# One visit instead of two for the state products of a chunk, and a copy of C shared by two engines, in a fused Mamba-2 and gated feed-forward kernel

## The chip, the cores and the metric

The kernel runs on one core of a Trainium2 chip. The metric is the device time of one execution in microseconds. The core has five engines that work at the same time, each through its own queue in order: TensorE (PE in the profile; its weight loads are listed as PEld), VectorE (DVE), ScalarE (ACT), GpSimd (POOL) and SyncE (SP), which issues the DMAs. They wait for one another through semaphores. Matrix products go to PSUM[...]; VectorE and ScalarE read them from there.

## The reference, cut to what matters

A state-space scan over 4 sequences with 8 heads, 768 steps, head size 32 and state size 16 feeds a feed-forward stage over 3072 tokens of width 256, whose middle has 2048 columns. All values are float32.

```
for each chunk of the sequence, with la = log(clip(a)), cum = cumsum(la):
    M       = (C @ B.T) * exp(cum_i - cum_j) * causal
    y       = M @ x  +  (C @ state) * exp(cum_i)
    state   = exp(sum la) * state + sum_j (B_j x_j) * exp(cum_last - cum_j)
X   = y laid out as (tokens, heads * head_dim)
h   = X @ w_in
out = (h * cos(h)) @ w_out
```

## The kernel before, in words

The sequences are cut into six chunks of 128 steps. Chunks 0 and 1 of this cut are handled in half chunks of 64 steps at the start (functions that end in `0` or `_unit`); chunks 2 to 5 are handled whole by `turn2`, `intra2`, `masked`, `open2`, `finish2` and `carry`. In the text, chunk c means one of these whole chunks.

The feed-forward stage sets the pace. It runs in 96 steps n, 16 for each chunk (`NF = 16`); step n of chunk n // 16 takes 256 columns of the middle layer for half of the tokens. One step is a chain through four engines:

- `first(n)`, L725 (8 matmul records): `hp` = y times `w_in`, into a PSUM bank.
- `wind_k(n)`, L732 on ScalarE, and `wind_w(n)`, L738 on VectorE: the argument of the cosine, reduced to one period. Both read `hp`.
- `gate(n)`, L747 on ScalarE: the cosine. `gated(n)`, L752 on VectorE: `gT` = `hp` times the cosine. It is the last reader of `hp`.
- `differ(n)`, L777, L779, L780 on GpSimd: differences of `gT` for a seven-product scheme; then `second(n)`, L834 (14 matmul records): products with `w_out`, summed in PSUM. It is issued two steps later (`LAG = 2`).

`hp` has two PSUM buffers of its own from step 4 on (`bank([P, TB], "hp", tag)` with tag "h" and `bufs=2`): step n writes the buffer of step n - 2, so `first(n)` can start only when `gated(n - 2)` is done.

The order on each engine is the order of the calls in the program (`manual_schedule`): nothing is moved by a scheduler, and an instruction that waits holds all behind it on its engine. In the loop over n (L1067) one turn issues `first(n)`, `wind(n)`, `gate(n)`, then `gated(n)` with some scan work for VectorE before or behind it (the list `behind`), then what TensorE does for the scan, with `second(n - 2)` in between.

The scan work of chunk c is spread over the 16 steps ahead of it. Called by step within those 16:

- steps 8 and 12: `intra2` (L621), the products C times B of two sequences each, into two PSUM tiles of two banks (`pair`, tag "scan", `bufs=2`), and `masked` for one sequence (L640: four VectorE products of these with the decays).
- steps 9 and 13: `masked` for the other sequence, the first entry of `behind`; it stands ahead of `gated` of its step.
- step 14: `open2(c)`, L651 and L659, after `second(12)`: the old state times C into the y tiles, and the sums for the new state. Its y tiles are the same two `pair` buffers. Chunk 5 has no L659, since no chunk comes after it.
- step 15: `finish2(c)`, L675, between `first(15)` and `second(13)`: the masked products times x, added in the y tiles; then `yT` is copied out by ScalarE (L682), and `carry` (L697 on VectorE, L701 on GpSimd) makes the new state.
- the next step, `first` of chunk c's own step 0, reads `yT`.

So TensorE's order around the change, with the step within the 16, is: `first(14)`, `second(12)`, `open2`, `first(15)`, `finish2`, `second(13)`, then `first` of the next chunk. `open2` and `finish2` use small tiles of the array (`tile_position`), the feed-forward products the whole of it.

In the set-up of chunk 0, C is loaded by four DMAs into `c4`, GpSimd copies it in another order of elements into `c0` (L365, 128 partitions x 512 elements), TensorE transposes `c0` in four parts (L417), and ScalarE takes the transposes out of PSUM (L421); the first products C times B (L478) follow. `c0[:, r]` is the operand of the transpose r.

Of the kernel before, what the change touches and what calls it, by code (L numbers as in the profile page):

```python
# [25 lines left out]
def kernel(  # L26
# [13 lines left out]
    V, ACT, G, PE = nc.vector, nc.scalar, nc.gpsimd, nc.tensor  # L40
# [31 lines left out]
    def pair(name):  # L72

        return psum.tile([P, 2, 4 * P], FP32, tag="scan", bufs=2, name=name)
# [44 lines left out]
    c4 = both[0][:, 1].rearrange("p (h r) n -> p h r n", h=H)  # L119
# [23 lines left out]
    def group(q, b):  # L143
        return slice(32 * (q ^ b % 2), 32 * (q ^ b % 2) + 32)
# [52 lines left out]
    def load_along(c, seqs=range(NB)):  # L197
# [5 lines left out]
        for b in seqs:  # L203
            for q in range(4 if b % 2 else 1):
# [9 lines left out]
                      in_=a[:, :, 0:P].rearrange("b h (k i) -> (b h) k i", k=2))  # L214
# [85 lines left out]
    for s in range(2):  # L300
# [3 lines left out]
        out=a_in, in_=a.rearrange("(u b) h (c p) -> (b h c) u p", u=NU, p=P))  # L304
# [52 lines left out]
    for p in range(2):  # L357
# [4 lines left out]
                  in_=mine.unsqueeze(2).to_broadcast([P, H, N]))  # L362
    c0 = loads.tile([P, 2, 2, 4, 2, N], FP32, tag="blocks", name="c0").rearrange(
        "p a b c d n -> p (a b c d n)").rearrange("p (r h n) -> p r h n", r=4, h=H)
    G.tensor_copy(out=c0.rearrange("p r h n -> p h r n"), in_=c4)  # L365
    G.memset(lead, 0.0)
    G.memset(lead[:, :, 0:1], 1.0)
    slot = const.tile([P, 2], FP32, name="slot")
# [275 lines left out]
    def open2(c):  # L644

        ys[c] = y = [pair("y") for _ in range(2)]
        for u in range(2):
            for s in range(2):
                for q in range(4):
                    r, p = group(q, s), 64 * (q % 2)  # L650
                    PE.matmul(y[s][p:p + 64, q // 2, u * P:(u + 1) * P],  # L651
                              lhsT=state[c - 1, u][r, s].rearrange("p t d -> p (t d)"),
                              rhs=part[c, u][2][r, s], start=(u == 0), stop=False,
                              tile_position=(r.start, p), skip_group_check=True)
        for b in range(NB if c < NC - 1 else 0):
            x_, sc = raw[c][1], scaled.pop((c, b))
            for q in range(4):
                two_, r = slice(2 * q, 2 * q + 2), group(q, b)
                PE.matmul(y[0][r, 0, (4 + b) * W:(5 + b) * W],  # L659
                          lhsT=sc[:, two_].rearrange("p h n -> p (h n)"),  # L660
                          rhs=x_[:, b, two_].rearrange("p h d -> p (h d)"), start=False, stop=True,
                          tile_position=(0, r.start), skip_group_check=True)

    def finish2(c):

        xr, y = raw[c][1], ys.pop(c)
        for late in (1, 0):
            i = slice(W, P) if late else slice(0, W)
            for u in range(2):
                for t in range(2):  # L670
                    for s in range(2):
                        b, m = 2 * u + s, part[c, u][1][s]
                        js = slice(0, P) if late else slice(s * W, s * W + W)
                        for q in range(4):
                            PE.matmul(y[s][32 * q:32 * q + 32, t, u * P + i.start:u * P + i.stop],  # L675
                                      lhsT=xr[js, b, 4 * t + q], rhs=m[js, 4 * t + q, i],
                                      start=False, stop=True, tile_position=(js.start, 32 * q),
                                      skip_group_check=True)
        yT[c] = two.tile([P, 2, TB], FP32, tag="yT", name="yT")
        to_ = yT[c].rearrange("p t (u s i) -> p t s u i", u=2, s=2)  # L680
        for s in range(2):
            ACT.copy(out=to_[:, :, s],  # L682
                     in_=y[s][:, :, 0:2 * P].rearrange("p t (u i) -> p t u i", u=2))
        for u in range(2):
            del part[c, u]
            if c < NC - 1:
                carry(c, u, y[0][:, 0, 4 * W:].rearrange("p (u s d) -> p u s d", u=2, s=2)[:, u])

    def carry(c, u, s_ps):


        state[c, u] = new = states.tile([P, 2, 2, D], FP32, tag="state", name="state")
        mask = slot.unsqueeze(1).unsqueeze(3).to_broadcast([P, 2, 2, D])
        whole = scan.tile([P, 2, 2, D], FP32, tag="whole", bufs=1, name="whole")
        old = state.pop((c - 1, u))
        for s in range(2):
            V.scalar_tensor_tensor(out=whole[:, s], in0=old[:, s],  # L697
                                   scalar=reach[c, u][:, s, P - 1:P],
                                   in1=s_ps[:, s].rearrange("p (t d) -> p t d", t=2),
                                   op0=ALU.mult, op1=ALU.add)  # L700
        G.tensor_tensor(out=new, in0=whole, in1=mask, op=ALU.mult)  # L701
# [39 lines left out]
    def wind(n):  # L741
        wind_k(n)
        wind_w(n)
# [172 lines left out]
    take_s0, _ = finish0(0)  # L916
# [47 lines left out]
    def units_at(n, i):  # L964
        return [k for k, at in unit_at.items() if at[i] == n]
# [38 lines left out]
    def ends(n):  # L1004
        return [(c, us) for c, at, us, _, _, end in plan if at + end == n]
# [61 lines left out]
    for n in range(AHEAD, NC * NF + LAG):  # L1067
        c, f = divmod(n, NF)
        if n < NC * NF:

            if c > 0 and f == (NJ if c == 1 else 0):
                if c == 1:
                    load(2, only=(x,))
                load(c + 2)
            if n in (NF - 4, NF + 1):
                for b in range(2):
                    load_a(2, (2 * (n > NF) + b,))
                    load_along(2, (2 * (n > NF) + b,))
            first(n)
            wind(n)  # L1080
            for at in pairs(n):
                turn2(*at)
            for k in units_at(n, 2):
                turn_unit(k)
            if n + 1 in piece:
                rests_of.append(grade(*piece[n + 1], later=True))
            gate(n)
            while len(rests_of) > (n == AHEAD):
                rest = rests_of.pop(0)
                if rest:  # L1090
                    rest()
            joins = n in piece and piece[n] in held
            if joins:
                join(*piece[n])

            behind = [lambda at=at: halved(*at) for at in halves_at(n)]
            behind += [lambda k=k, p=p: decays0(k, p) for k, at in unit_at.items()
                       for p in range(2) if at[0][p] == n]
            behind = [lambda at=(c, 2 * u + 1): masked(*at) for c, u in pairs(n - 2)] + behind
            behind = [lambda k=k: weights(k, 1) for k in units_at(n - 1, 3)] + behind  # L1100
            if not joins and behind:
                behind.pop(0)()
            gated(n)
            if add_s and (n == NF - 5 or units_at(n - 1, 4)):
                add_s()
                add_s = None
            for do in behind:
                do()
            if f not in (10, 11):
                for do in unsummed:  # L1110
                    do()
                unsummed.clear()
            for k, ((_, last_), *_) in unit_at.items():
                if last_ == n:
                    weigh0(k)
                    if k == 3:
                        units_of_decay()
        for i, js in differ_at.get(n, ()):
            differ_w(i, js)
        for c, _ in ends(n - 1):  # L1120
            finish2(c)
            raw.pop(c)
        if n == AHEAD + 1:
            second(AHEAD - LAG)
        if n >= LAG and n != AHEAD:
            second(n - LAG)
        for c, u in pairs(n - 1):
            intra2(c, u)
            masked(c, 2 * u)
        for k in units_at(n, 3):  # L1130
            for t in range(2):
                inner(k, t)
            weights(k, 0)
        for k in units_at(n, 4):
            take_s, add_s = finish0(k)
            take_s()
        for k in units_at(n, 1):
            reach_unit(k)
        for c, _ in ends(n):
            open2(c)  # L1140
        for c, u in pairs(n + 1):
            for b in (2 * u, 2 * u + 1):
                reaches(c, b)
                load_along(c + 1, (b,))
            turn_blocks(c, u)
        for at, (c, u) in block_loads.items():
            if at == n:
                loading = load_blocks(c, u)
            if at <= n < at + 6:
                next(loading)  # L1150
# [30 lines left out]
```

## Time and profile before

| what | value |
|---|---|
| time, median of 3 runs | 371.13 us (370.97 to 371.22) |
| time of the profiled execution | 371.16 us |
| its span, first to last instruction | 369.4 us |
| PE busy / PEld busy | 362.5 us (98%) / 325.0 us (88%) |
| DVE / ACT / POOL busy | 276.9 (75%) / 172.2 (47%) / 213.4 us (58%) |
| L725 `hp` matmuls, x768 | 183.2 us busy |
| L752 `gT`, x96 | 680 ns each |
| L640 `m`, x64 | 411 ns each (median) |

The span is what the trace covers; the time has 1.8 us more around it. A line of a timeline gives start, length, engine, line of code, operation, tile written and tiles read, and, in brackets, how long the engine was idle before it and what ended that. A line of the chain of waits gives start, length and engine of one piece of the chain that ended last. TensorE matmuls overlap one another by a part of their length, so distances between starts say more than lengths.

### The profile page before, as it was taken

What the parts mean: (1) busy time and instruction counts of PE and PEld (TensorE: products, weight loads), DVE (VectorE), ACT (ScalarE), POOL (GpSimd) and SP (SyncE); (2) the same over time, 40 slices, a digit from 0 to 9 for tenths busy, and PEclk for the clock granted to TensorE, in tenths of its full rate; (3) what the DMA queues carried; (4) which work ended last, traced back from release to release, by engine and by line L of the source; (5) the groups of instructions that cost most, each with busy time, mean ns of one, the idle gap of its engine ahead of it and who ended that gap; (6) DMA issues with size and microseconds to landing.
All of it is one profiled execution on the core that took longest, in us unless ns stands there. A gap on an engine that the chain in (4) does not pass through costs nothing.

```text
span 369.4 us, 9265 instructions
## 1 busy us (share of the span) xinstructions
PE 362.5 (98%) x3646; PEld 325.0 (88%) x3646; DVE 276.9 (75%) x451; ACT 172.2 (47%) x299; POOL 213.4 (58%) x336
## 2 busy tenths in 40 slices
PE   7999999999999999999999999999999999999995
PEld 5688888888999889899989999889999988999995
DVE  7789998578699857978876987776887783543463
ACT  2697766453445244354344344434434534444442
POOL 6567757579784456665446674544675344554451
PEclk9999999999999999999999999999999999999999
DMA  9996957257226736631055341020010010010011
GB/s 135 244 381 134 224 114 100 44 147 185 72 78 90 139 106 91 196 107 34 6 80 113 92 129 44 1 52 5 18 23 0 2 30 2 2 29 2 0 30 30
DMA packets 97708, 30.60 MB, mean 83 GB/s; under 512 B 71456, under 2 KB 93568, under 8 KB 97664
## 3 DMA queue, kind: packets, MB, share of 16 engines
q1 hardware_dynamic: 95376, 29.55, 35.0%
q10 hardware_dynamic: 2288, 0.46, 0.8%
q8 instruction: 29, 0.48, 0.5%
q14 instruction: 15, 0.12, 0.1%
HBM read 26.58 MB, written 3.34 MB: 81 GB/s over the span
## 4 chain that ended last, share of the span: by engine, by line
PE 92%; DVE 3%; ACT 2%; issue 1%; ACTq 0%; DVEq 0%
PE hp L725 43%; PE o L834 34%; PE o L796 6%; PE y L675 2%; PE g L621 2%; DVE mag L279 1%; PE g L478 1%; DVE lam L397 1%; PE warm L84 1%; PE y L651 1%; PE y L520 1%; DVE mag L281 1%; PE y L503 1%; DVE w L738 1%; PE a_ps L386 1%
## 5 line engine op out<-in xcount | busy, mean ns | idle before, releaser
L725 PE MATMUL hp<-yT,w_in 128*128 128x256 f32 x768 | 183.2, 382 | 0.4 <-DVE gT L752 0.3
L725 PEld LDWEIGHTS hp<-yT,w_in 128*128 128x128 f32 x768 | 139.4, 190 | 19.5 <-issue 2.3
L777 POOL TENSOR_TENSOR gd<-gT 128x256 f32<-128x256 f32 x79 | 59.9, 758 | 99.9 <-DVE gT L752 86.8
L747 ACT ACTIVATE w<-w,quarter 128x512 f32<-128x512 f32 x96 | 69.2, 721 | 84.4 <-DVE w L738 84.3
L738 DVE SCALAR_TENSOR_TENSOR w<-hp,k 128x512 f32<-128x512 f32 x96 | 65.8, 685 | 44.3 <-ACT k L732 43.9
L732 ACT ACTIVATE k<-hp 128x512 int32<-128x512 f32 x96 | 57.0, 594 | 83.2 <-PE hp L725 82.9
L752 DVE TENSOR_TENSOR gT<-hp,w 128x512 f32<-128x512 f32 x96 | 65.3, 680 | 33.2 <-ACT w L747 21.7
L834 PE MATMUL o<-words,gd 128*128 128x128 f32 x474 | 66.0, 275 | 0.0
L834 PEld LDWEIGHTS o<-words,gd 128*128 128x128 f32 x474 | 59.3, 192 | 0.3 <-POOL gd L779 0.2
L834 PEld LDWEIGHTS o<-w_out,gT 128*128 128x128 f32 x316 | 47.2, 191 | 4.2
L834 PE MATMUL o<-w_out,gT 128*128 128x128 f32 x316 | 48.4, 276 | 0.0
L779 POOL TENSOR_TENSOR gd<-gT,gd 128x128 f32<-128x128 f32 x79 | 44.0, 556 | 6.2
L780 POOL TENSOR_TENSOR gd<-gT,gd 128x128 f32<-128x128 f32 x79 | 43.3, 548 | 6.2
L580 DVE TENSOR_TENSOR_SCAN lam<-arow,unit 128x512 f32<-128x512 f32 x32 | 42.7, 1333 | 0.0
L834 PE MATMUL o<-words,gT 128*128 128x128 f32 x158 | 30.6, 275 | 0.0
L834 PE MATMUL o<-w_out,gd 128*128 128x128 f32 x158 | 30.5, 275 | 0.0
L796 PE MATMUL o<-w_out,gT 128*128 128x256 f32 x128 | 29.9, 379 | 0.0
L796 PEld LDWEIGHTS o<-w_out,gT 128*128 128x128 f32 x128 | 24.2, 190 | 3.3
L640 DVE TENSOR_TENSOR m<-g,lam 128x256 f32<-128x256 f32 x64 | 24.7, 414 | 0.4
L834 PEld LDWEIGHTS o<-words,gT 128*128 128x128 f32 x158 | 24.0, 192 | 0.0
L834 PEld LDWEIGHTS o<-w_out,gd 128*128 128x128 f32 x158 | 24.0, 192 | 0.0
L851 DVE TENSOR_TENSOR sum<-ps,sum 128x256 f32<-128x256 f32 (+1 forms) x27 | 16.7, 645 | 0.6
(111 smaller groups left out, 279.2 us busy)
## 6 DMA issues: line engine op xcount, KB each, us to landing
arow<-a_cut SPq DMA_DIRECT2D x16, 512.0 KB
words<-in_moe_w_in_dram SPq DMA_DIRECT2D x8, 512.0 KB
words<-in_moe_w_out_dram SPq DMA_DIRECT2D x8, 512.0 KB
out_dram<-sum SPq DMA_DIRECT2D x18, 128.0 KB
xr<-in_x_dram SPq DMA_DIRECT2D x16, 128.0 KB
xr<-in_x_dram SPq DMA_DIRECT2D x16, 64.0 KB
bc<-in_B_dram SPq DMA_DIRECT2D x15, 64.0 KB
arow<-a_cut SPq DMA_DIRECT2D x2, 256.0 KB
```

The costliest lines, as they stand in the source:

```text
L580: V.tensor_tensor_scan(out=lam[c, b][:, hs].rearrange("p h i -> p (h i)"), data0=rows_.rearrange("p h i -> p (h i)"), data1=unit[:, b % 2 ...
L640: V.tensor_tensor(out=m_[js, :, :, is_], in0=g_[js, :, :, is_], in1=l_[js, :, :, is_], op=ALU.mult)
L725: PE.matmul(to_[:, e], lhsT=w_in[:, k, fs], rhs=y[:, k], start=(k == 0), stop=(k == KT - 1), skip_group_check=True)
L732: ACT.activation(k, hp[n], AF.Copy, bias=0.25, scale=INV_2PI)
L738: V.scalar_tensor_tensor(out=w, in0=hp[n], scalar=INV_2PI, in1=k, op0=ALU.mult, op1=ALU.subtract)
L747: ACT.activation(cos, cos, AF.Sin, bias=quarter, scale=TWO_PI)
L752: V.tensor_tensor(out=gT[n], in0=hp.pop(n), in1=cos, op=ALU.mult)
L777: G.tensor_tensor(out=d[:, 0:2], in0=g[:, 1:2].to_broadcast([P, 2, P]), in1=g[:, 3::-3], op=ALU.subtract)
L779: G.tensor_tensor(out=d[:, 2], in0=g[:, 0], in1=d[:, 0], op=ALU.subtract)
L780: G.tensor_tensor(out=d[:, 3], in0=g[:, 2], in1=d[:, 2], op=ALU.subtract)
L796: PE.matmul(o[c, u][:, t], lhsT=g[:, 2 * e + t], rhs=w_out[:, 2 * j + e], start=(j == e == t == 0), stop=(j == NJ - 1 and e == 1), skip_gr ...
L834: PE.matmul(at[q], lhsT=a_[q], rhs=w[q], start=(j == 0 and q in starts), stop=(j == NJ - 1), skip_group_check=True)
```

## The change

Two edits.

1. In chunk 0's set-up, the copy `c4` to `c0` is cut in two along r: GpSimd copies r = 0 and 1, ScalarE r = 2 and 3 (128 x 256 elements each).
2. In the loop, `open2(c)` is called one step later, directly ahead of `finish2(c)`: TensorE's order becomes `first(14)`, `second(12)`, `first(15)`, `open2`, `finish2`, `second(13)`. This holds for chunks 2 to 5, four times in all. What `open2` computes, its tiles and buffers, and the order on the other engines stay as they are.

```diff
-    G.tensor_copy(out=c0.rearrange("p r h n -> p h r n"), in_=c4)
+    G.tensor_copy(out=c0[:, 0:2].rearrange("p r h n -> p h r n"), in_=c4[:, :, 0:2])
+    ACT.copy(out=c0[:, 2:4].rearrange("p r h n -> p h r n"), in_=c4[:, :, 2:4])
...
         for c, _ in ends(n - 1):
+            open2(c)
             finish2(c)
             raw.pop(c)
...
-        for c, _ in ends(n):
-            open2(c)
```

## The prediction, on record before the change was run

> **What bounds the kernel now.** I read the page first, then the chain of waits, then the timeline of each engine around the places that are edited. Part 1 of the page:
>
> ```profile
> PE 362.5 (98%) x3646; PEld 325.0 (88%) x3646; DVE 276.9 (75%) x451; ACT 172.2 (47%) x299; POOL 213.4 (58%) x336
> ```
>
> TensorE is the bound, and the chain is TensorE alone from 34.79 us to the end but for splinters. So a TensorE instruction saved is time saved, and a TensorE wait added is time lost. The chain around one visit (chunk 3; start, length):
>
> ```profile
> 183.77 1.73 PE hp L725 x8
> 185.50 1.56 PE o L834 x14
> 187.06 0.62 PE y L651 x32
> 187.68 0.58 PE y L659 x32
> 188.26 1.92 PE hp L725 x8
> 190.19 1.82 PE y L675 x117
> 192.01 1.76 PE o L834 x14
> 193.76 1.30 PE hp L725 x6
> ```
>
> In order: `first(14)`, `second(12)`, `open2` (L651, L659), `first(15)`, `finish2` (L675), `second(13)`, `first` of the next chunk. See that an hp or o block costs 1.73 or 1.56 us, but 1.92 and 1.76 us when small-tile products came just before it: 0.19 and 0.20 us more for each return to the full array, twice a chunk. That is what one visit can save.
>
> Then I asked whether `first(15)` could start where `open2` starts now. Its PSUM buffer is freed by `gated(13)`. VectorE in the same stretch:
>
> ```profile
> 183.12 1.40 DVE L640 TENSOR_TENSOR m<-g,lam 128x256 f32<-128x256 f32 x4
> 184.44 0.67 DVE L738 SCALAR_TENSOR_TENSOR w<-hp,k 128x512 f32<-128x512 f32 x1
> 185.04 1.74 DVE L640 TENSOR_TENSOR m<-g,lam 128x256 f32<-128x256 f32 x4
> 186.81 0.69 DVE L752 TENSOR_TENSOR gT<-hp,w 128x512 f32<-128x512 f32 x1
> 187.42 0.68 DVE L738 SCALAR_TENSOR_TENSOR w<-hp,k 128x512 f32<-128x512 f32 x1
> ```
>
> These are `masked` of the third sequence, w of step 13, `masked` of the fourth, `gated(13)`, w of step 14. `gated(13)` ends at 186.81 + 0.69 = 187.50 us. VectorE has no idle time between 180.25 and 188.1, so it is late by its own load (before these come four L851 sums, 2.3 us). TensorE ends `second(12)` at 187.06: today `open2` fills the time until the buffer is free, and `first(15)` finds it free 0.7 us before its start.
>
> What such a wait looks like is seen once, at the end of the start phase:
>
> ```profile
> 33.97 0.68 DVE L752 TENSOR_TENSOR gT<-hp,w 128x512 f32<-128x512 f32 x1
> 34.79 1.97 PE L725 MATMUL hp<-yT,w_in 128*128 128x256 f32 x8 [0.34 <-DVE gT L752]
> ```
>
> hp starts 0.14 us after gT's end at 34.65, and its block takes 1.97 us from idle. (A second case: gT ends at 151.45, hp starts at 151.60.)
>
> The first edit concerns this stretch:
>
> ```profile
> 6.62 0.61 POOL L365 COPY c<-bc 128x512 f32<-128x512 f32 x1 [0.84 <-DMA bc<-in_C_dram]
> 7.29 0.66 PE L417 MATMUL tp<-ident,c 128*128 128x128 f32 x4 [0.50 <-POOL c L365]
> 7.98 0.84 ACT L421 ACTIVATE cT<-tp,slot 128x256 f32<-128x256 f32 x2 [3.33 <-DVE lam L397]
> 8.71 0.37 ACT L432 COPY turned<-tp 128x256 f32<-128x256 f32 x1
> 9.14 0.73 PE L478 MATMUL g<-cT,turned 32*64 32x128 f32 x32 [0.54 <-ACT turned L432]
> ```
>
> The copy waits for C, the transposes for the copy, and ScalarE has stood idle for 3.3 us when the transposes end at 7.95. The page names DVE lam (ended 7.96) as what released ScalarE; the code has ScalarE need only `slot`, done at 4.0, and the transposes, so I take it as a coincidence.
>
> **What the Trainium skill says.** "TensorEngine Tiling (Array Packing)", Key Properties: changing the tiling mode, as opposed to the tile, drains TensorE. The trace agrees: the 0.19 and 0.20 us above. "Perfetto Trace Analysis", Optimizing Tensor Performance, Matmuls: independent groups should rotate through different PSUM banks so that the evacuation of one overlaps the matmuls of the next. Here hp rotates through two, and the overlap lasts only while VectorE is less than two steps behind; 34.79 shows it end. "TensorE: Matmul & The Clock Gate", Why this matters for your kernels: idle gaps above about 3 us lower the clock. The gaps that I forecast are near 1 us, and the granted clock is 1.00 in all four stretches around the visits, so I charge nothing for it. "ScalarE: Activation LUTs", What ACT_TABLE_LOAD costs: an ACTIVATE with immediate scale and bias takes 186 ns + 0.833 ns per element, an estimate of 0.40 us for 256; the trace has 0.37 us for L432 of that shape.
>
> **The change, part by part.**
>
> *Merging, without any wait.* Chunk 3 takes from the end of `second(12)`: 1.20 (open2) + 1.92 + 1.82 + 1.76 = 6.70 us. In the new order hp follows a full-array block and costs 1.73: 1.73 + 1.20 + 1.82 + 1.76 = 6.51. Gain 0.19 us a chunk, 0.8 us for four.
>
> *The wait it adds.* `first(15)` would start near 187.06 but has to wait for `gated(13)`: 187.50 + 0.14 = 187.64. From there 1.97 + 1.20 + 1.82 + 1.76 ends at 194.39, against 193.76: 0.63 us lost. Queued behind the waiting hp on TensorE are `open2`, `finish2` and `second(13)`, all of which could run but stand behind it. The lower bound: read by starts, hp at 187.50 + 0.06 (a shorter release; L651 in chunk 2 resumes 0.07 us after the VectorE product that it waits for), then 1.73, 0.10 to enter the small tiles, 1.20, 1.82 and 1.66 give 194.07 against hp at 193.60: 0.47. I take 0.56.
>
> *Chunk 4* has the same times 58.12 us later (`gated(13)` ends at 245.62, the next chunk's hp starts at 251.72): 0.47 to 0.63, I take 0.56.
>
> *Chunk 5* has no L659. `gated(13)` ends at 303.75; 303.89 + 1.97 + 0.62 + 1.82 + 1.76 = 310.06 against 309.44 in the chain: 0.62, by starts 0.48; I take 0.55. Here hp starts today 0.14 us after gT: its 0.62 us of L651 lies wholly in time that TensorE would otherwise wait.
>
> *Chunk 2*: `gated(13)` ends later, at 129.00, since VectorE comes in with more scans. 129.14 + 1.97 + 1.20 + 1.82 + 1.76 = 135.89 against 135.13: 0.76, by starts 0.62; I take 0.69. That `open2` today waits 0.32 us within itself, for a y buffer that `masked` frees at 128.28, is in these figures: in the new order that wait is gone, covered by the longer one.
>
> Sum: 0.69 + 0.56 + 0.56 + 0.55 = 2.36 us, bounds 2.04 to 2.64.
>
> *What else moves.* VectorE, ScalarE, GpSimd and SP keep their order. After `finish2` ScalarE copies yT (1.05 us); k and the cosine of step 15 are now done before `finish2` ends, so the copies start at once and end some 1.2 us after `second(13)` starts, which lasts 1.66: covered, with about 0.3 us to spare after the 0.14 us release. `masked` of the fourth sequence is done at 186.78 in chunk 3 (128.28 in chunk 2), before hp can start, so `finish2` doesn't wait for it. The `sc` buffers that L659 now frees later are next written at 198.18 (L563 on GpSimd): no one waits. `open2` issues no DMA; the loads of x and B that reuse buffers wait for `finish2`, as before. One recovery is possible: in chunk 2's own steps hp stalls by 0.18 us at 151.60 (gT late) and an o block by 0.26 us behind it; VectorE is paced by hp there, so I give nothing, and keep -0.4 for the range.
>
> *The shared copy.* GpSimd takes 0.29 us for 128 elements (L361) and 0.61 for 512, so by the line between them 0.40 for 256; ScalarE 0.37 to 0.40, and it is free from 4.65 on. Both wait for the same C. Both halves are done at 6.62 + 0.40 = 7.02, not 7.23: 0.21 us earlier. From there to 34.79 the chain runs through the first products, VectorE and ScalarE, with ScalarE and VectorE rather than a transfer ending nearly every wait (the one DMA wait, ACT for the first weights at 9.32, is 0.2 us). I take 0.20 of gain, bounds 0 (DVE lam was the true releaser, or the gain is lost in the weight conversion up to 34.79) and 0.25. A loss is excluded within 0.05 us, as both copies are shorter than the one they replace.
>
> Total: 2.36 - 0.20 = +2.16 us. The profiled run took 371.16 (span 369.4 and 1.8 around it), which agrees with the median 371.13 within 0.03: **373.3 us**, slower by 0.6%.
>
> **The rivals.** *The wait isn't there* (faster). It would need `gated(13)` done 0.14 us before `second(12)` ends, at 186.92 rather than 187.50, 0.58 us earlier. For it: VectorE is paced by k of earlier steps, and TensorE changes its order. Against it: the order changes only after VectorE's work in question has its inputs, and VectorE is busy without a break from 180.25. Then 4 x 0.19 + 0.20 = 0.96 is gained: 370.2 us. The break-even is hp at about 187.2 in chunk 3. *The wait is partly regained*: the next chunk's stalls vanish (0.44 us in chunk 2) and the later visits have VectorE 0.4 us earlier relative to TensorE, so that each loses 0.1: 0.3 + 3 x 0.1 - 0.2 = +0.4: 371.5 us. Against it: VectorE waits for k in each chunk, so it follows TensorE. *A further wait behind the visit*: hp of the next chunk waits for yT because the copies start late; each 0.4 us beyond the spare 0.3, four times: 373.3 + 1.6 = 374.9. Against it: ScalarE has nothing else to do at that time.
>
> **How the numbers follow.** Forecast 0.80; wait not there 0.09; partly regained 0.05; further wait 0.06. A measurement of this kernel tells about 0.2% (0.74 us) from no change. The forecast's own bounds: low 2.04 - 0.25 - 0.4 = +1.4, 372.5; high 2.64 with no gain at the start and 0.07 us more release for each, +2.9, 374.1. With a little to the lower side for a partial recovery, the range is 372.3 to 374.1. Slower 0.86, within 0.2% 0.05, faster 0.09.
>
> **What would show it.** In the profile after: hp of step 15 in chunks 2 to 5 with an idle time before it ended by DVE gT, near 0.6 us in chunks 3 to 5 and 1.3 us in chunk 2; L651, L659 and L675 in one block; PE's busy time lower by about 0.8 us with a longer span; the transposes L417 near 7.08. The forecast is wrong if hp of step 15 starts within 0.1 us of the end of `second(12)`, or if the distance between the hp starts around a visit (8.27 us from `second(12)` to the next chunk's hp in chunk 3) becomes shorter.

## The result, and the profile after

The changed kernel takes 375.71 us (median of 6 runs, 374.36 to 378.85), the kernel before 371.06 us (6 runs, 370.83 to 371.77). The ratio is 1.0131, with an interval of 1.0092 to 1.017: slower, as forecast, but by 4.65 us where 2.2 us were forecast, and outside the range of 372.3 to 374.1 us. The profiled execution took 375.99 us with a span of 374.1 us, and the span is what is taken apart below. After the change the lines of the code stand one lower (hp is L726, gT L753, `open2` L652 and L660, `finish2` L676, `second` L835), since the copy takes two lines, L365 and L366.

Part 1 of the page after:

```profile
PE 361.9 (97%) x3646; PEld 324.7 (87%) x3646; DVE 275.7 (74%) x451; ACT 173.0 (46%) x300; POOL 217.6 (58%) x336
```

TensorE has 0.6 us less to do and the span is 4.7 us longer. So the loss is idle time. What TensorE waits for, in us in total, times and longest, stands in the table of waits (the three largest lines):

```profile
PE hp L726 <- DVE gT L753: 3.3, 5, 1.2
PE y L676 <- issue: 1.7, 1, 1.7
PE hp L726 <- issue: 1.4, 1, 1.4
```

The first line is the forecast wait: four visits, and the fifth is the one at the end of the start phase, which was there before. The other two lines were not forecast. "issue" means that the profile shows nothing that TensorE waited for.

The chain around chunk 3's visit, after (start, length, piece):

```profile
188.06 0.70 DVE gT L753
188.77 0.14 issue
188.90 1.96 PE hp L726 x8
190.87 0.62 PE y L652 x32
191.49 0.58 PE y L660 x32
192.07 1.68 PE y L676 x117
193.76 1.76 PE o L835 x14
195.51 1.73 PE hp L726 x8
```

Read it against the chain of before: `open2` and `finish2` are one block now, one of the two dear returns to the full array is gone, and the chain leaves TensorE for `gated(13)`, which ends 0.14 us before hp starts. VectorE in the same stretch is the same row of work as before, still without a gap:

```profile
186.31 1.72 DVE L641 TENSOR_TENSOR m<-g,lam 128x256 f32<-128x256 f32 x4
188.06 0.69 DVE L753 TENSOR_TENSOR gT<-hp,w 128x512 f32<-128x512 f32 x1
188.67 0.68 DVE L739 SCALAR_TENSOR_TENSOR w<-hp,k 128x512 f32<-128x512 f32 x1
```

Where the rest went is seen in the timeline of TensorE around chunk 2's visit:

```profile
128.59 1.97 PE L726 MATMUL hp<-yT,w_in 128*128 128x256 f32 x8 [1.24 <-DVE gT L753]
130.48 0.69 PE L652 MATMUL y<-rT,state 32*64 32x128 f32 x32
131.10 0.65 PE L660 MATMUL y<-xr,sc 128*32 128x64 f32 x32
131.57 1.87 PE L676 MATMUL y<-m,xr 128*32 128x64 f32 x128
...
135.03 0.60 PE L726 MATMUL hp<-yT,w_in 128*128 128x256 f32 x2
137.00 1.24 PE L726 MATMUL hp<-yT,w_in 128*128 128x256 f32 x5 [1.36 <-issue]
```

and around chunk 5's:

```profile
306.07 1.97 PE L726 MATMUL hp<-yT,w_in 128*128 128x256 f32 x8 [0.56 <-DVE gT L753]
307.96 0.69 PE L652 MATMUL y<-rT,state 32*64 32x128 f32 x32
308.59 1.81 PE L676 MATMUL y<-m,xr 128*32 128x64 f32 x118
312.12 0.33 PE L676 MATMUL y<-m,xr 64*32 64x64 f32 x10 [1.73 <-issue]
312.38 0.71 PE L835 MATMUL o<-w_out,gT 128*128 128x128 f32 x4
```

TensorE stops in the middle of a block: once between the second and the next of eight hp products that all have the same inputs, once ten products before the end of `finish2`. No tile can be late there, as the instructions in front had the same tiles or tiles of the same age. I call such a stop a hole. In the kernel before the same two blocks run through (chunk 2's hp, chunk 5's `finish2`):

```profile
134.97 1.89 PE L725 MATMUL hp<-yT,w_in 128*128 128x256 f32 x8
...
305.79 1.89 PE L675 MATMUL y<-m,xr 128*32 128x64 f32 x128
```

The transfers show what was on its way. Page part 3 has two queues of the kind "instruction", in both kernels alike. One has 15 packets of 8 KB (q14). The other is:

```profile
q8 instruction: 29, 0.48, 0.5%
```

29 packets, 0.48 MB, so about 16 KB each. That this queue serves TensorE is worked out below, from the number of its packets. The view of transfers, narrowed to 308.9 to 309.9 us in the kernel after, shows one of them and nothing else:

```profile
DMA packets 1, 0.02 MB, mean 16 GB/s; under 512 B 0, under 2 KB 0, under 8 KB 0
q8 instruction: 1, 0.02, 7.7%
```

By the trace's own records this packet runs from 309.43 to 310.66, and the one before chunk 2's hole from 134.49 to 135.44. Counted from the start of the program in TensorE products and weight loads, TensorE has issued 2965 when the one packet ends, and it stops at number 2965; it has issued 6496 when the other ends, and it stops at 6496. The holes end 1.56 and 1.46 us after the packets' ends. In the kernel before the packets at the same places (130.80 to 131.84, and 304.71 to 305.78) came with work left, and TensorE worked on through both: it came to number 2965 as late as 3.6 us after the first one's end. But in chunk 5 it reached number 6496 only 1.56 us after the packet's end, which is no later than the holes' ends above.

The start phase has a smaller stop of the same kind in the kernel before too, in the middle of the products of L503 (table of waits, before):

```profile
PE y L503 <- issue: 0.4, 1, 0.4
```

It stands at instruction 441, and TensorE goes on at 16.34 us, 1.98 us after the first packet's end. In the kernel after it lasts 0.09 us and ends at 15.77.

Set out by the starts of hp, after minus before, the last hp starts 4.77 us later (the span is 4.74 us longer):

| stretch | forecast us | measured us |
|---|---|---|
| start, up to the first hp behind it (34.79 to 34.22) | -0.20 | -0.57 |
| from there to chunk 2's visit | 0 | +0.03 |
| chunk 2, wait for `gated(13)` | +0.69 | +0.61 |
| chunk 2, hole | 0 | +1.52 |
| chunk 2's own steps, stalls that vanish (in E1 too, so not by the visit) | 0 | -0.31 |
| chunk 3, wait | +0.56 | +0.47 |
| chunk 4, wait | +0.56 | +0.46 |
| chunk 5, wait (the value that E4 has for it without a hole) | +0.55 | +0.59 |
| chunk 5, hole (the rest of 2.56) | 0 | +1.97 |
| sum | +2.16 | +4.77 |

The four waits cost 2.13 us, the two holes 3.49 with what they bring about in their stretch (1.36 and 1.73 us idle).

### The profile page after: what moved, and what is told of

The parts are those of the page before. It is cut to its first block, busy times and chain, and to the rows that moved or that the text cites. A ratio compares the mean times of both kernels' runs of the same rounds, so it can differ in the third digit from the quotient of the medians.

```text
span 374.1 us, 9259 instructions
## 1 busy us (share of the span) xinstructions
PE 361.9 (97%) x3646; PEld 324.7 (87%) x3646; DVE 275.7 (74%) x451; ACT 173.0 (46%) x300; POOL 217.6 (58%) x336
## 4 chain that ended last, share of the span: by engine, by line
PE 73%; DVE 14%; ACT 4%; issue 4%; DMA 2%; POOL 1%; SPq 1%; DVEq 0%; ACTq 0%; POOLq 0%
PE hp L726 35%; PE o L835 25%; PE o L797 6%; DVE m L641 3%; DVE gT L753 2%; DMA xr<-in_x_dram 2%; DVE sum L852 2%; PE y L676 2%; DVE w L739 2%; DVE reach L572 1%; ACT w L748 1%; DVE turned L595 1%; ACT k L733 1%; DVE mag L279 1%; PE g L622 1%
## 5 line engine op out<-in xcount | busy, mean ns | idle before, releaser
L726 PE MATMUL hp<-yT,w_in 128*128 128x256 f32 x768 | 183.2, 382 | 4.6 <-DVE gT L753 3.3
L726 PEld LDWEIGHTS hp<-yT,w_in 128*128 128x128 f32 x768 | 139.5, 190 | 23.9 <-issue 5.0
L753 DVE TENSOR_TENSOR gT<-hp,w 128x512 f32<-128x512 f32 x96 | 65.2, 680 | 33.1 <-ACT w L748 21.7
L835 PE MATMUL o<-words,gd 128*128 128x128 f32 x474 | 66.0, 275 | 0.0
L835 PEld LDWEIGHTS o<-words,gd 128*128 128x128 f32 x474 | 59.3, 192 | 0.1
L781 POOL TENSOR_TENSOR gd<-gT,gd 128x128 f32<-128x128 f32 x79 | 47.8, 605 | 6.2
L835 PEld LDWEIGHTS o<-w_out,gT 128*128 128x128 f32 x316 | 47.2, 191 | 4.1
L835 PE MATMUL o<-w_out,gT 128*128 128x128 f32 x316 | 48.4, 276 | 0.0
L780 POOL TENSOR_TENSOR gd<-gT,gd 128x128 f32<-128x128 f32 x79 | 44.0, 556 | 6.2
L835 PE MATMUL o<-words,gT 128*128 128x128 f32 x158 | 30.6, 275 | 0.0
L835 PE MATMUL o<-w_out,gd 128*128 128x128 f32 x158 | 30.5, 275 | 0.0
L835 PEld LDWEIGHTS o<-words,gT 128*128 128x128 f32 x158 | 24.0, 192 | 0.0
L835 PEld LDWEIGHTS o<-w_out,gd 128*128 128x128 f32 x158 | 24.0, 192 | 0.0
```

Source lines behind the costliest of these rows:

```text
L726: PE.matmul(to_[:, e], lhsT=w_in[:, k, fs], rhs=y[:, k], start=(k == 0), stop=(k == KT - 1), skip_group_check=True)
L753: V.tensor_tensor(out=gT[n], in0=hp.pop(n), in1=cos, op=ALU.mult)
L780: G.tensor_tensor(out=d[:, 2], in0=g[:, 0], in1=d[:, 0], op=ALU.subtract)
L781: G.tensor_tensor(out=d[:, 3], in0=g[:, 2], in1=d[:, 2], op=ALU.subtract)
L835: PE.matmul(at[q], lhsT=a_[q], rhs=w[q], start=(j == 0 and q in starts), stop=(j == NJ - 1), skip_group_check=True)
```

## The experiments

Two theories. **Instruction supply**: the merged visit issues 384 TensorE instructions (192 product records and as many weight loads; 320 in all in chunk 5) within 3 us, faster than the packets on q8 bring them, and TensorE runs dry at a block boundary that falls at a bad place; the forecast wait for `gated(13)` comes on top. **Something in the visit itself** (a semaphore, a buffer, a drained queue that the profile doesn't name): then the holes belong to the code of the visits, and stay with it when instructions are added elsewhere. E1 and E2 part the two edits, E3 takes the wait away, E4 and E6 shift the instruction stream, E8 thins it, and E5, E7, E9 try which order is best. Diffs are against the changed kernel unless said otherwise.

### E1 and E10: the shared copy alone

The kernel before, with edit 1 only.

```diff
-    G.tensor_copy(out=c0.rearrange("p r h n -> p h r n"), in_=c4)
+    G.tensor_copy(out=c0[:, 0:2].rearrange("p r h n -> p h r n"), in_=c4[:, :, 0:2])
+    ACT.copy(out=c0[:, 2:4].rearrange("p r h n -> p h r n"), in_=c4[:, :, 2:4])
```

> Only the shared copy of C, open2 at its old place. Both theories: the gain of the start alone, 0.2 to 0.55 us, 370.5 to 370.9 us; the first hp after the start phase near 34.3 to 34.6 instead of 34.79; no idle time of TensorE around the visits beyond what the kernel before has.

> The shared copy alone once more, beside the version before this on the same chip: 370.4 to 370.8 us; the time when the first x lands (10.6 to 11.1 us so far) sets how much of the start's gain is kept.

Measured: 370.59 us against 371.13, ratio 0.999 (0.9982 to 0.9997), and again 370.86 against 371.17, ratio 0.9994 (0.9985 to 1.0004). By the medians the copy is worth 0.3 to 0.5 us, but the second comparison can't tell it from nothing. E1's table of waits has no hole at the visits. Its `finish2` of chunk 5 takes 2.13 us where 1.89 was usual, though, with a stop of 0.2 us at 306.80, 1.4 us after a packet's end (305.42): the order of before is near the edge there. The copies cost what was forecast; the timeline of the kernel after:

```profile
6.19 0.41 ACT L366 COPY c<-bc 128x256 f32<-128x256 f32 x1 [1.51 <-DMA bc<-in_C_dram]
7.36 0.84 ACT L422 ACTIVATE cT<-tp,slot 128x256 f32<-128x256 f32 x2 [0.77 <-PE tp L418]
```

The second line also settles a question of the prediction: ScalarE is now released by the transposes and not by DVE lam, so that releaser was a coincidence, as I had taken it (the same scan ends at 7.96 here too, 0.6 us after ScalarE's start). What the start is worth in one execution varies, by the start of the first hp behind it: -0.57 us in the kernel after, -0.52 in E1, -0.27 in E5, -0.07 in E9, and +0.23 in E3 with the same copy; E2, which has the old copy, has +0.13. One part of it, from the timeline of TensorE after:

```profile
10.76 0.37 PE L513 MATMUL y<-xr,sc 64*32 64x64 f32 x20 [0.21 <-DMA xr<-in_x_dram]
```

A transfer, the first load of x, now ends a wait there. It landed at 10.71 us in this execution and at 11.03 in E3. But a later stop has the last word in most runs: the one at instruction 441 (L504 here; 0.09 us idle in the kernel after, none in E5, 0.28 to 0.64 in the others named). TensorE passes it at 16.34 us before, 15.77 after, 15.80 in E1, 16.04 in E5, 16.25 in E9, 16.56 in E3 and 16.47 in E2, which is 1.4 to 2.0 us after the first packet's end, and in all of them the first hp behind the start follows 18.45 to 18.48 us later. So the start's end follows this packet as well as the copy, and what the copy is worth can't be read from one execution.

E1 gains elsewhere too: 0.31 us in chunk 2's own steps, where the visit is as before. E10 and all other runs with the shared copy show the same, and E2, which lacks it, doesn't. Why it goes with the copy isn't shown.

### E2: the visit alone

Edit 2 without edit 1 (the copy as in the kernel before).

```diff
-    G.tensor_copy(out=c0[:, 0:2].rearrange("p r h n -> p h r n"), in_=c4[:, :, 0:2])
-    ACT.copy(out=c0[:, 2:4].rearrange("p r h n -> p h r n"), in_=c4[:, :, 2:4])
+    G.tensor_copy(out=c0.rearrange("p r h n -> p h r n"), in_=c4)
```

> Only open2 moved behind hp, the copy of C as before. Theory 1 (the loss is the wait of hp for gated(13) alone): +0.5 to +0.7 us for each of four visits, 373.1 to 373.6 us, and the 1.4 and 1.7 us of idle time without a named cause in the changed kernel were a matter of one execution. Theory 2 (besides it TensorE runs out of instructions, because a visit in one piece consumes more than one 16 KB block of 256 instructions in less time than a block needs to arrive): the same two holes as in the changed kernel, at chunk 2's first hp and in chunk 5's L676, each 1 to 2 us, since TensorE's stream of instructions is the same: 375.5 to 376.5 us.

Measured: 376.49 us (6 runs), ratio 1.0149 (1.0116 to 1.0181). So the loss is the visit's. The waits for gT are 1.21, 0.54, 0.54 and 0.56 us, and the same two holes are there: 1.09 us at instruction 2965 and 1.74 us at 6496, after packets that end at 136.24 and 311.72. That two programs on two executions stop at the same two numbers speaks for supply, but not yet against the code, since both have the same visits.

### E3: `gated(13)` ahead of `masked`

The wait is taken away: at step 13 VectorE makes gT first and `masked` of the fourth sequence after it.

```diff
-            if not joins and behind:
+            late = any(u == 1 for _, u in pairs(n - 2))
+            if not joins and behind and not late:
                 behind.pop(0)()
             gated(n)
```

> The changed kernel, but in step 13 gated(13) goes ahead of masked of the fourth sequence on VectorE, so that hp of step 15 finds its buffer free. Theory 1: the wait was all of the loss, so the time goes below the kernel before, by the merging (4 x 0.19) and the start (0.2 to 0.5): 369.9 to 370.3 us. Theory 2: no idle time before hp of step 15, but the holes inside the visits of chunks 2 and 5 stay at 1 to 2 us each, or grow, as the visit comes sooner after the fetch was asked for: 372 to 374 us.

Measured: 372.36 us (14 runs), ratio 1.0031 (1.0019 to 1.0043). The waits for gT are gone in chunks 3 to 5, and 0.39 us is left in chunk 2, where gT itself waits for the cosine. Chunks 3 and 4 now gain 0.33 us each, by the starts of hp around the visit, where they lost 0.47 and 0.46: that is what one return to the full array and no wait are worth. But chunk 5 loses 1.76 us. Its timeline of TensorE in E3:

```profile
302.75 1.89 PE L726 MATMUL hp<-yT,w_in 128*128 128x256 f32 x8
304.58 0.69 PE L652 MATMUL y<-rT,state 32*64 32x128 f32 x32
305.20 1.79 PE L676 MATMUL y<-m,xr 128*32 128x64 f32 x117
308.73 0.33 PE L676 MATMUL y<-m,xr 64*32 64x64 f32 x11 [1.74 <-issue]
```

hp has no wait ahead of it, and the hole is still there, just as long, at instruction 6495, after a packet that ends at 307.45. So wait and hole are two separate costs. In chunk 2 the packet began 1.84 us earlier (132.65), took 1.97 us and so ended 0.82 us earlier, and the hole shrank to 0.27 us.

### E4: 48 TensorE instructions more, far ahead of the visits

One product of the warm-up at the very start is replaced by 13 small ones; what the kernel computes is untouched, since nothing reads them. Each of these products shows as two product and two weight-load records, so the stream is 48 TensorE instructions longer.

```diff
-    fill(bank([P, 2, P], "warm", "o"), 1)
+    warm = bank([P, 2, P], "warm", "o")
+    for _ in range(13):
+        PE.matmul(warm[0:32, 0, 0:16], lhsT=ones[:, 0:32], rhs=ones[:, 0:16], start=True,
+                  stop=True, tile_position=(0, 0), skip_group_check=True)
```

> The changed kernel with 48 more TensorE instructions in the warm-up (13 products of 32 x 16 in place of one of 128 x 256), so that every block boundary of the instruction stream falls 48 instructions earlier in each visit. Theory 1: nothing changes but the start, by some tenths of a us; holes, if any, where they were. Theory 2: the holes move. Chunk 5's (the block before begins 48 instructions into its visit) goes, chunk 2's stays and lies 48 instructions earlier, in second(13) or at the end of L676, and chunk 3 may get one (its boundary comes to the end of the visit); each hole with a 16 KB packet of TensorE's instruction queue that starts 2 to 3 us ahead of its end.

Measured: 381.55 us (4 runs), ratio 1.0285 (1.0268 to 1.0301). Its timeline of TensorE at the start, in chunk 2 and in chunk 5:

```profile
23.43 1.78 PE L726 MATMUL hp<-yT,w_in 128*128 128x256 f32 x7 [3.45 <-issue]
...
137.06 1.80 PE L676 MATMUL y<-m,xr 128*32 128x64 f32 x121
140.50 0.31 PE L676 MATMUL y<-m,xr 64*32 64x64 f32 x7 [1.65 <-issue]
...
316.11 1.89 PE L676 MATMUL y<-m,xr 128*32 128x64 f32 x128
```

Three answers. Chunk 2's hole has moved in the code, from an hp of the next chunk back into `finish2`, but not in the stream: it stands at instruction 2966, beside 2965 before. Chunk 5's hole is gone, with the same visit in the same order. And a new hole of 3.45 us has appeared in the start phase, among products that the change never touched, at instruction 696, after a packet from 21.04 to 22.13; I had not expected it, and it is a third of the 10.3 us by which the span is longer than before. (The first hp behind the start is 4.9 us late in all; ten products of L387 near 5 us take 4.03 us, before 3.02. In chunk 2 slow products follow the hole, as in E6 below.) The small stop of the start phase is at 441 as before, though the code has moved: it now falls after 4 of the 32 products of L504, where it fell after 28 of them. A hole that stays at its number while the code moves past it is one of the instruction stream. Between the packets of the holes at 696 and 2966 lie nine packets, and 2270 instructions; between those at 2965 and 6496 fourteen, and 3531. That is 252 each, with a few instructions that are neither product nor weight load left out of the count.

This can be held against all traces. The m-th packet goes with number 192 + 252 m: 441 to 444, 696, 2965 and 6496 belong to packets 1, 2, 11 and 25. In none of the twelve traces does TensorE begin at such a number less than about 1.3 us after the end of its packet, and all holes at and behind the visits end 1.3 to 1.6 us after it. So each packet brings the very next block, and a hole lasts from the moment at which TensorE runs out until 1.3 to 1.6 us after the packet's end.

### E6: the same shift inside the loop

12 small products at step 20, ahead of all four visits (their result is overwritten by the step's own products).

```diff
+        for _ in range(12 if n == NF + 4 else 0):
+            PE.matmul(hp[n][0:32, 0:16], lhsT=ones[:, 0:32], rhs=ones[:, 0:16], start=True,
+                      stop=True, tile_position=(0, 0), skip_group_check=True)
```

> The changed kernel with 48 more TensorE instructions (12 products of 32 x 16) in one step of chunk 1, ahead of all visits and behind the start phase. They cost 0.7 to 1.5 us by themselves. Theory 1: the time of the changed kernel and that cost, 376.4 to 377.2 us, holes where they were. Theory 2: no hole in the start phase, chunk 5's hole gone (-2.0 us), chunk 2's at 1.4 to 1.8 us and 48 instructions earlier, at the end of L676: 374.6 to 375.6 us.

Measured: 377.3 us (4 runs), ratio 1.016 (1.0144 to 1.0175). The start is left alone and has no hole; chunk 5's hole is gone again, and its visit costs 0.59 us; chunk 2's has moved into `finish2` again, at instruction 2966:

```profile
132.87 1.80 PE L676 MATMUL y<-m,xr 128*32 128x64 f32 x121
136.54 0.31 PE L676 MATMUL y<-m,xr 64*32 64x64 f32 x7 [1.88 <-issue]
136.78 0.89 PE L838 MATMUL o<-w_out,gT 128*128 128x128 f32 x4
137.47 1.49 PE L838 MATMUL o<-words,gd 128*128 128x128 f32 x6
```

The places came as expected, the time not: 374.6 to 375.6 us was. The last line above holds the reason. Six products take 1.49 us, where in the kernel after they take 0.83. The table by windows of E6 has the granted clock, a mean over each window, as the third number from the end:

```profile
130.00:134.60 4.60, 4.60 (x193) 3.76 (x193) 3.05 (x5) 2.04 (x3) 3.94 (x6) 1.00 0.29 74
136.54:139.00 2.46, 2.46 (x19) 2.37 (x20) 0.47 (x2) 0.58 (x1) 1.12 (x3) 0.63 0.64 154
139.00:142.00 3.00, 3.00 (x14) 2.66 (x14) 0.00 (x0) 0.00 (x0) 0.00 (x0) 0.73 0.11 25
142.00:146.00 4.00, 4.00 (x30) 3.79 (x30) 2.40 (x3) 1.92 (x3) 1.14 (x2) 1.00 0.65 66
```

By the trace's records of the clock it is 0.50 from 137.18 to 140.59 us, which the second and third window mix with 1.00. So the hole costs its length and then, by an estimate from these figures, half of 3.4 us, 1.7 us of slow products. E4 has the same from 140.97 to 144.38 us.

### E8: a visit with fewer instructions

Two of each four products of `finish2` are left out, so that half of M times x is missing from the output; the visit issues 128 TensorE instructions fewer.

```diff
-                        for q in range(4):
+                        for q in range(0, 4, 2):
```

> The changed kernel with half of finish2 left out (heads 0 and 2 of each four alone), so that a visit has 256 TensorE instructions and not 384; the output lacks half of the products M x. Theory 1: the waits of hp stay, the holes stay, and the time falls by the work left out, 4 x 0.84: about 372.3 us. Theory 2: the waits of hp stay at 0.54 to 1.2 us, but with no more than one block boundary in a visit there is no hole: about 368.8 us.

Measured, in one run beside the kernel before (370.99 us): 371.66 us, span 369.9. There are 27 packets in place of 29: 2 fewer for 512 instructions fewer in four visits, or 256 for each packet, so the queue is TensorE's. The four waits for gT stay (1.21, 0.55, 0.53 and 0.54 us) and there is no hole at a visit (the small stop at 441 is there, 0.35 us). The size of the saving was wrong: I had expected 368.8, because I took half of `finish2`'s 1.7 us as saved; the half that is left still takes 1.65 us, so some 0.2 us a visit was saved. That fits products on different tiles of the array running side by side, so that leaving some out leaves the others as long as they were; no run tests this by itself. This run thins the burst and also moves the later boundaries; it agrees with supply, but alone it would not decide.

### E5 and E7: what goes with what

E5 is E3 with chunk 5's `open2` back at its old place, to lose the last hole; E7 puts `open2` back in all four chunks and keeps `gated(13)` first. The diff of E7 against E3 (E5 has the same with a test for the chunk):

```diff
         for c, _ in ends(n - 1):
-            open2(c)
             finish2(c)
...
+        for c, _ in ends(n):
+            open2(c)
```

> gated(13) ahead of masked as before this, the shared copy, and open2 behind hp for chunks 2 to 4 alone; in chunk 5, whose hole was the long one, open2 stands at its old place. Theory 2 (wait and instruction supply): no hole in chunk 5, the small one of chunk 2 (0.3 us) stays, chunks 3 and 4 gain 0.3 us each from the merging: 370.0 to 370.4 us, below the kernel before and near or below the copy alone (370.6). Theory 1 (wait alone) gives about the same, 369.8 to 370.2; against both stands that the merging gains nothing, 370.6 or more.

> The shared copy and gated(13) ahead of masked, with open2 at its old place in all chunks. Both theories: hp of step 15 finds its buffer free in either order, so no change against the copy alone: 370.4 to 370.8 us; chunk 2 may lose up to 0.4 us if open2 waits longer for its y buffer, which masked of the fourth sequence frees, and finds it 0.8 us later here.

Measured: E5 371.65 us, ratio 1.0016 (1.0008 to 1.0023); E7 377.53 us, ratio 1.0183 (1.016 to 1.0207). Both miss what I expected, 370.0 to 370.4 and 370.4 to 370.8. The timeline of TensorE in E7, chunk 3:

```profile
188.32 0.45 PE L652 MATMUL y<-rT,state 32*64 32x128 f32 x8 [0.51 <-DVE m L641]
189.22 0.67 PE L652 MATMUL y<-rT,state 32*64 32x128 f32 x24 [0.45 <-DVE m L641]
```

`open2` writes y tiles whose PSUM buffers `masked` of the fourth sequence is still reading, and with gT first that is later. Each visit lost 1.4 us or more; in E5 chunk 5's visit lost 1.44 by the same wait, while chunks 3 and 4 kept their gain of 0.33. I had the buffers in my own description of the kernel and did not carry them through. So each of the two moves alone loses: `gated(13)` first helps only with `open2` behind hp, and `open2` behind hp only with `gated(13)` first.

### E9: the best of both

Copy shared; in chunks 2 to 4 `gated(13)` first and `open2` behind hp; chunk 5, whose boundary falls badly, entirely as before.

```diff
-            if not joins and behind:
+            late = any(u == 1 and c_ < NC - 1 for c_, u in pairs(n - 2))
+            if not joins and behind and not late:
                 behind.pop(0)()
...
         for c, _ in ends(n - 1):
-            open2(c)
+            if c < NC - 1:
+                open2(c)
             finish2(c)
...
+        for c, _ in ends(n):
+            if c == NC - 1:
+                open2(c)
```

> The shared copy; in chunks 2 to 4 gated(13) ahead of masked and open2 behind hp; in chunk 5 both orders as in the kernel before. By the readings so far: start -0.3 to -0.55, chunk 2 0 to +0.3 with its small hole and -0.3 regained behind it, chunks 3 and 4 -0.33 each, chunk 5 without wait and hole: 369.7 to 370.1 us. If instead chunk 5 has a hole in this order too, or its open2 waits for a y buffer, 371 us or more.

Measured: 370.28 us (9 runs) against 371.17, ratio 0.9971 (0.9958 to 0.9983): faster than both kernels, by less than expected (369.7 to 370.1), as the start gave only 0.07 us in its profiled execution. Against the copy alone, run beside it (E10, 370.86 us), it is 0.6 us faster. Chunk 2 gains 0.20 us and then 0.32 in its own steps, chunks 3 and 4 gain 0.33 each, and chunk 5 is even. The margin is thin: in chunk 2 the packet ends at 133.75 and TensorE reaches number 2965 at 135.14, 1.4 us later and without a hole. Chunk 3's visit in E9, with no bracket behind either hp, and 6.37 us from one to the other:

```profile
186.32 1.89 PE L726 MATMUL hp<-yT,w_in 128*128 128x256 f32 x8
188.14 0.69 PE L652 MATMUL y<-rT,state 32*64 32x128 f32 x32
188.76 0.65 PE L660 MATMUL y<-xr,sc 128*32 128x64 f32 x32
189.23 1.86 PE L676 MATMUL y<-m,xr 128*32 128x64 f32 x128
191.03 0.71 PE L835 MATMUL o<-w_out,gT 128*128 128x128 f32 x4
...
192.69 1.89 PE L726 MATMUL hp<-yT,w_in 128*128 128x256 f32 x8
```

## Why the prediction was right and wrong

**The wait it adds: right.** hp of step 15 waits for `gated(13)` in all four visits, starts 0.14 us after it, and has in front of it 1.24 us idle in chunk 2 and 0.56 to 0.57 in the others, where 1.3 and near 0.6 were foretold. E3 takes exactly this away, by making gT earlier. The rival that the wait isn't there is refuted: VectorE did not run ahead. The four waits cost 2.13 us of 2.36 forecast. Chunks 2 to 4 stand at the lower bounds (0.61, 0.47, 0.46 beside 0.62, 0.47, 0.47): the bound read by starts was the better measure, because small-tile blocks overlap at both ends and `finish2` behind `open2` takes 1.68 us in the chain instead of 1.82. That they agree to 0.01 us is luck in part: that bound had set 0.06 us for the release, which took 0.14.

**Merging, without any wait: right in kind, mis-sized.** The forecast was 0.19 us a chunk; E3 and E9 show 0.33. The term left out is that same shorter `finish2`: 0.14 us is what the chain has between 1.82 and 1.68.

**The wrong step: "What else moves".** It went through engines, buffers and the transfers that the code issues, said that `open2` issues no DMA, and priced the merged visit as the sum of its old blocks. It never asked where TensorE's instructions come from. The page before listed the queue (q8, 29 packets), and I read it as no part of the change, though the change packs 384 instructions into one piece that had been cut in two by an hp of 1.9 us. The two holes cost 3.49 us, more than the whole forecast. Without them the profiled execution would stand at 375.99 - 3.49 = 372.5 us, at the low end of the range. That is arithmetic; the run nearest to it is E8, with the waits and no hole: its 371.66 us and some 0.2 us for the work left out of each visit make 372.5 as well.

The Trainium skill does speak of it: "Runtime: NRT & Kernel Launch", Instruction fetch mechanics, says that an engine's instruction memory is refilled in blocks of 16 KiB, 256 instructions, and that crossing a boundary is mostly hidden. The packet size agrees (0.48 MB in 29 packets, 252 counted instructions each). "Mostly hidden" agrees for the kernel before, where the 0.4 us at instruction 441 are all that its table of waits shows, but not for a burst of small tiles: here a crossing cost 0.27 to 1.88 us in and behind the visits, and 3.45 us once in the start phase. The measurement decides.

**A further rival, "a further wait behind the visit": wrong in mechanism.** It forecast 374.9 us by a late yT. The time came near that, but yT was not late: in chunk 3 ScalarE's copies end at 194.80 and hp starts at 195.35.

**"I charge nothing" for the clock: right for the profiled execution, wrong for others.** I had set the forecast gaps of 1 us against the 3 us of "TensorE: Matmul & The Clock Gate", Why this matters for your kernels. In E4 and E6 two gaps whose starts lie 6 us apart, 1.20 to 1.23 us and then 1.65 or 1.88, were followed by a clock of 0.50 for 3.4 us; in the profiled execution after, 1.24 and 1.36 us, 8.3 us apart, were not, and neither was E4's single hole of 3.45 us in the start phase (its clock is 1.00 up to 140.97 us). So the page's 3 us hold in neither direction here, and whether the length or the distance of the two gaps counts was not tested. In two of the six runs of the changed kernel (376.31 and 378.85 us) the mean granted clock was 0.994, near E4's 0.996 and E6's 0.995, and 0.999 in the profiled execution; that the same drop lengthened those two is likely, but they have no trace. One of the 21 runs of E10 has such a mean too (0.995, 373.3 us), with the visits as before.

**The shared copy: right in mechanism, mis-sized in one execution.** The profiled execution gained 0.57 us, with a bound of 0.25. The copies took 0.41 and 0.40 us as forecast, but C itself was there 0.4 us earlier in that execution (GpSimd's copy started at 6.21, before at 6.62), which is no part of the change. "ScalarE and VectorE rather than a transfer" failed: two transfers stand behind the copy, the first load of x, whose landing varies by some 0.3 us, and then the first packet of instructions, which lets TensorE go on at instruction 441. By the medians the copy gives 0.3 to 0.5 us, of which the traces put 0.31 into chunk 2's own steps and the rest, which varies, into the start.

**The partial recovery: near in size, by luck.** Chunk 2's own stalls vanished and gave 0.31 us back; I had kept 0.4 for it in the range and nothing in the sum. But the reason, a visit that comes later, is wrong: E1 and E10 show the same 0.31 without it, and E2, with the visit and without the shared copy, shows none. The further 0.1 us for each later visit did not come.

What stays open: why a packet starts when it does. In the trace the request is not seen, only the transfer. Chunk 2's hole had five lengths (0.27, 1.09, 1.36, 1.65, 1.88 us), and they follow from the packet's end: it came 1.01, 0.23 and 0.19 us ahead of the stop in E3, E2 and the kernel after, and 0.16 and 0.52 us behind it in E4 and E6. That a larger distance between packet and need would close the hole was not tried by itself.

## What to carry to other kernels

Small-tile products use up TensorE's instructions far faster than large ones (here 384 in 3.0 us, against 44 in 3.3 us for an hp and an o block), so before joining two bursts of them, count their products and weight loads against the packets of the instruction queue: a pause by a large-tile block in between can be what hides the refill. A hole with no releaser, in the middle of products with the same inputs, which ends shortly after such a packet and keeps its instruction number when the code is shifted, is a refill, and it can come up in an untouched place when a few instructions are added ahead, as it did once here (E4). And a step put behind a buffer that another engine frees needs that engine's order changed with it: here each of the two moves alone lost, 1.5% (E2, its holes included) and 1.8% (E7), and both together gained in chunks 2 to 4 where there was no hole (E9).

## What was not expected of the hardware

- TensorE ran dry for 1.09 to 1.88 us at a block of its instruction stream in and behind bursts of 320 to 384 instructions in 3 us (0.27 us where the packet came early), and for 3.45 us once in the start phase (E4). The longer holes ended 1.3 to 1.6 us after the end of a 16 KB packet on q8, which itself took 0.9 to 1.3 us, with no other transfer under way in chunk 5.
- A stop of the same kind stands at instruction 441 in the start phase, up to 0.64 us long and in the kernel before too; the first hp behind the start follows it by 18.45 to 18.48 us.
- 13 tiny products in place of one at the start made the changed kernel 5.8 us slower (381.55 beside 375.71), with a hole of 3.45 us that had not been there.
- Half of the products of `finish2` left out saved some 0.2 of 1.9 us.
- Two gaps of 1.2 us and of 1.65 to 1.88 us, whose starts lie 6 us apart, were followed by a granted clock of 0.50 for 3.4 us (E4, E6), while one gap of 3.45 us left it at 1.00 (E4).
